# Stage A of a Fourier and MoE kernel by radix 2: folds spread over product groups, burst behind the inverse

## Chip, cores and metric

The kernel runs on one core of a Trainium2 chip. The metric is device time in microseconds (us) of one execution, the median of several runs. An execution has five engines that take their own instructions in order: TensorE (PE in the rows; PEld is its loading of weights), VectorE (DVE), ScalarE (ACT), GpSimd (POOL) and SyncE (SP), which here only issues DMA transfers.

## What is computed

```python
X = np.fft.rfft(x, axis=1)                     # x: 8 batches x 3008 x 256
Yr = Xr @ w_r - Xi @ w_i + b_r
Yi = Xr @ w_i + Xi @ w_r + b_i
Y = softshrink(Yr, 0.01) + 1j * softshrink(Yi, 0.01)
y = np.fft.irfft(Y, n=3008, axis=1)            # 24064 tokens x 256
h = y @ w_in                                   # 256 -> 2048
out = (h * np.cos(h)) @ w_out                  # 2048 -> 256
```

## The kernel before

Every batch of 3008 = 64 x 47 rows goes through a Fourier part and then through the two big products (MoE). The MoE of batch b is 6 tiles of 512 tokens by 16 steps; a step (`moe_step`) makes six matmuls of 512 columns into a PSUM bank `ph` (L937 to L939), passes it through ScalarE and VectorE (`u`, `gh`, `gl`), and three steps later (`SKEW`) `second` makes six more (L919, L920, L923) from `gh` and `gl`. `gl = u - gh` is a subtraction on GpSimd in every second step (`POOL_GL`, L331) and on VectorE in the others (L334).

Between these steps the Fourier part of batch b + 1 is woven in. The generators yield costs in paced units; `pull` takes as many units per step as `share(b)` grants, from sums written out by hand (`COST`, `A_COST`, `LAST`). So the position of each piece is set by the order of the generator `fourier(b)` and by the units of what stands before it. Tile's scheduler then orders each engine's instructions; `floor()` keeps an instruction behind the results of the step before last, and `burst()` keeps the matmuls of one group together and lets the first of them wait for all that the group needs.

One batch's Fourier part runs, for q = 0 to 3, through `combine(q)` (sums and splits into high and low parts), `wmix(q)` (the product with the weights: eight positions, of which six are matmul groups, `pw`, and two are turns, in which VectorE transposes what GpSimd has folded), `forward(q + 1)` (burst `pb`), and `inverse(q - 1)` (burst `pi`, 16 matmuls of 24 rows by 32 columns by 512, each recorded as two passes). At q = 1 to 3 there also stands a group of stage A of the batch after that (`stage_a(b + 1)`, batches 2 to 7, so 18 groups in all): it takes two loads `xt` of 128 x 1024 from DRAM, which GpSimd's queue issues (L448), and does a 64-point transform across partitions.

Stage A before: GpSimd makes for each load a sum `xe` (L460) and, in place, a difference (L461), each 128 x 512. `folds` gives them out after the third position of `wmix`, but without `floor()` for batches over 2, so that the scheduler may run them as early as the load is there. The group (`burst_of`) is a burst `pa` of 8 matmuls of 64 rows by 64 columns by 512 into four PSUM banks; ScalarE copies each bank (`ao`), and SyncE's queue stores them to scratch (L465), from which the next batch's `forward` loads `at` (L565). The four products of one load stand on the four quarters of the 64 x 64 tiles, the two loads one behind the other. The group stands after position 5, the inverse after position 6. Batch 1's stage A runs in another way at the start and is not touched. The constants of stage A are columns 256 to 319 of `ff`.

Of the kernel before, what the change touches and what calls it, by code (L numbers as in the profile page):

```python
# [13 lines left out]
F32 = mybir.dt.float32  # L14
# [73 lines left out]

def _constants():
    n1, s = np.arange(64), np.arange(32)  # L90
# [26 lines left out]
    for sl in range(1, 32):  # L117
        for k2 in range(47):
            sig[sl, k2] = 1 if crt[sl, k2] <= N // 2 else -1
# [61 lines left out]
def tile_body(ctx: ExitStack, tc, x, w_r, w_i, b_r, b_i, w_in, w_out,  # L181
# [26 lines left out]
    def load_constants():  # L208
        with nc.allow_non_contiguous_dma(reason="bias"):
            for r, bsrc in enumerate((b_r, b_i)):  # L210
                nc.gpsimd.dma_start(bb[:, r, :], bsrc.rearrange("(c p) -> p c", p=128))
        ws["sig"] = pool["pro"].tile([96, 32], F32, name="sig", bufs=1)
        nc.gpsimd.dma_start(ws["sig"], c_sig)
        nc.gpsimd.dma_start(fi[0], c_if)
        ws["minus"] = wk.tile([128, 64], F32, tag="xe", name="minus", bufs=2)
        nc.gpsimd.tensor_scalar(out=ws["minus"], in0=ff[:, 256:], scalar1=-1.0, scalar2=None, op0=ALU.mult)
# [223 lines left out]
    def stage_a(b):  # L440
        scr1[b] = dr.tile([2, 24, 32, 2, 256], F32, tag="scr1", name=f"scr1_{b}")
        ld, ev = {}, {}
# [10 lines left out]
        def fold(c):  # L453
            with floor() if b == 2 else ExitStack():
                sums(c)

        def sums(c):
            ev[c] = wk.tile([128, 2, 256], F32, tag="xe", name="xe", bufs=2)
            lo, hi = ld[c][:, :, 0], ld[c][:, :, 1]
            nc.gpsimd.tensor_tensor(out=ev[c], in0=lo, in1=hi, op=ALU.add)  # L460
            nc.gpsimd.tensor_tensor(out=lo, in0=lo, in1=hi, op=ALU.subtract)  # L461

        def store(c, ao, after=None):
            for v in range(2):
                ins = nc.sync.dma_start(  # L465
                    scr1[b][v, 4 * c:4 * c + 4].rearrange("i s r d -> (s r) i d"),
                    ao[64 * v:64 * v + 64].rearrange("p (i d) -> p i d", i=4))
                if after is not None:
                    behind(ins, after.ins, "first tile")
# [7 lines left out]
        def burst_of(cs, banks=None, home=stage_out):  # L477
# [4 lines left out]
            if b == 1:  # L482
                ins = burst(1 if odd else 2, [((p[c, h][64 * v:64 * v + 64], (ws["minus"] if v * g else ff[:, 256:])[64 * h:64 * h + 64],
                            ld[c][64 * h:64 * h + 64, :, g]),
                           dict(start=g == 0, stop=g == 1, skip_group_check=True))
                          for c in cs for g in range(2) for h in range(2) for v in (1, 0)])
                if pro:
                    mark["fill"] = mark["pa"] = ins
            else:
                burst(len(ps2), [((p[c, h][64 * v:64 * v + 64], ff[64 * h:64 * h + 64, 256:320],  # L490
                                   (ld[c][64 * h:64 * h + 64, :, 0] if v else ev[c][64 * h:64 * h + 64])),
                                  dict(start=True, stop=True, skip_group_check=True))
                                 for c in cs for h in range(2) for v in (1, 0)])
            if banks:
                yield 0.0
            for c in cs:
# [11 lines left out]
                if b > 1:  # L508
                    del ld[c], ev[c]
                    load(c + 2)  # L510
            yield BURST

        def folds(j):
            for c in (2 * j, 2 * j + 1):
                fold(c)
                yield 0.5
# [14 lines left out]
        def begin():  # L531
            load(0)
            load(1)

        return SimpleNamespace(begin=begin, folds=folds, alone=alone, release=release, one=lambda *a: burst_of([a[0]], *a[1:]),
                               group=lambda j: burst_of([2 * j, 2 * j + 1]))


    def stage_b(b):
# [15 lines left out]
        def load(q):  # L555
            if b and q < 4:
# [4 lines left out]
                for h in range(4):  # L561
                    own = q == 0 and SLOT0[h] != SLOTS[h]
                    r0 = 64 * (h // 2) + 24 * (h % 2)
                    for (v, r), s0, s1 in ((SLOT0[h], 0, 1), (SLOTS[h], 1, 8)) if own else ((SLOTS[h], 0, 8),):
                        ins = nc.sync.dma_start(t[r0:r0 + 24, 256 * s0:256 * s1].rearrange("j (s d) -> j s d", d=256),  # L565
                                                scr1[b][v, :, 8 * q + s0:8 * q + s1, r])
# [257 lines left out]
    def fourier(b):  # L824
# [14 lines left out]
        if b == 1:  # L839
            yield from quiet()  # L840
            yield from on.forward(1)
        for q in range(4):
            mix = on.wmix(q)
            yield from take(mix, 2)
# [187 lines left out]
    A_COST = 3 * (1.0 + QUIET + 3 * READ + BURST)  # L1032
# [99 lines left out]
```

## Time and profile before

| | us |
|---|---|
| median of 3 runs (2570.58 to 2575.36) | 2571.95 |
| the profiled execution's own time | 2572.61 |
| span of the profiled execution, first to last instruction | 2570.8 |
| TensorE busy | 2548.1 |
| VectorE busy | 1858.0 |
| ScalarE busy | 1676.6 |
| GpSimd busy | 1029.5 |

Busy is the time in which at least one instruction of the engine runs. TensorE's matmuls are pipelined, so two of them overlap in the rows and the distance between starts is what one costs. In rows of busy time by stretch, each engine's us are followed by its count; the granted clock of 1.00 is full speed, and the last two columns are the DMA engines' share and GB/s.

### The profile page before, as it was taken

To read this page: it belongs to the slowest core of one execution; us is meant where nothing else is said; L and a number is where in the kernel's file an instruction comes from. 1 tells how busy PE (TensorE), PEld (TensorE's weight loads), DVE (VectorE), ACT (ScalarE), POOL (GpSimd) and SP (SyncE) were. 2 spreads that over 40 slices of the span, in tenths; PEclk is the share of its full clock that TensorE was granted. 3 is DMA by queue.
4 is the path that set the end of the run, shared out by engine and by line. 5 is a ranking of instruction groups with operands and counts; after the bars stand their busy time and mean duration, and the time that the engine had idled before them with its cause. 6 is when DMAs were issued, how large, how long until landed. Compare 5 with 4: busy or idle time off the path is not lost.

```text
span 2570.8 us, 42992 instructions
## 1 busy us (share of the span) xinstructions
PE 2548.1 (99%) x15961; PEld 2063.0 (80%) x15961; DVE 1858.0 (72%) x2909; ACT 1676.6 (65%) x3119; POOL 1029.5 (40%) x1002
## 2 busy tenths in 40 slices
PE   9999999999999999999999999999999999999999
PEld 7577778877788778887788777887788888888888
DVE  5887776877777777777767777677776777766665
ACT  5766666666666666666666666666676666666666
POOL 2135563555334552345524545244442444322222
PEclk9999999999999999999999999999999999999999
DMA  7545444444335443364423544335433343210000
GB/s 239 185 117 150 133 118 118 128 136 139 91 84 155 133 130 87 90 162 137 120 79 106 146 126 120 98 95 144 140 103 99 90 115 110 65 43 17 17 25 16
DMA packets 172954, 283.12 MB, mean 110 GB/s; under 512 B 15608, under 2 KB 114200, under 8 KB 169160
## 3 DMA queue, kind: packets, MB, share of 16 engines
q1 hardware_dynamic: 161896, 243.78, 33.8%
q0 software_dynamic: 10112, 35.53, 4.4%
q8 instruction: 126, 2.06, 0.3%
q10 hardware_dynamic: 736, 1.05, 0.1%
q14 instruction: 84, 0.69, 0.1%
HBM read 149.76 MB, written 130.55 MB: 109 GB/s over the span
## 4 chain that ended last, share of the span: by engine, by line
PE 84%; DVE 5%; DMA 3%; ACT 3%; issue 3%; POOL 2%; SPq 0%; ACTq 0%; DVEq 0%; POOLq 0%
PE ph L937 12%; PE po L919 12%; PE po L923 12%; PE po L920 12%; PE ph L938 12%; PE ph L939 12%; PE pw L676 2%; PE pw L678 2%; PE pw L677 2%; PE pc L383 1%; PE pb L383 1%; DVE u L951 1%; DMA xt<-in_dram 1%; PE pw L672 1%; DVE u L948 1%
## 5 line engine op out<-in xcount | busy, mean ns | idle before, releaser
L331 POOL TENSOR_TENSOR gl<-u,gh 128x512 fp32r<-128x512 f32 (+1 forms) x384 | 493.0, 1284 | 1088.6 <-ACT gh L952 931.7
L950 ACT ACTIVATE u<-u 128x512 f32<-128x512 f32 (+1 forms) x768 | 478.6, 623 | 351.2 <-DVE u L948 350.3
L948 DVE SCALAR_TENSOR_TENSOR u<-ph,u 128x512 f32<-128x512 f32 (+1 forms) x768 | 515.4, 673 | 263.8 <-ACT u L947 261.7
L951 DVE TENSOR_TENSOR u<-ph,u 128x512 f32<-128x512 f32 (+1 forms) x768 | 518.5, 675 | 246.6 <-ACT u L950 234.7
L952 ACT CAST gh<-u 128x512 fp32r<-128x512 f32 (+1 forms) x768 | 467.8, 609 | 214.7 <-DVE u L951 211.0
L947 ACT ACTIVATE u<-ph 128x512 int32<-128x512 f32 (+1 forms) x768 | 448.4, 586 | 244.1 <-PE ph L939 234.3
L937 PE MATMUL ph<-xTh,win 128*128 128x512 f32 (+1 forms) x1536 | 600.9, 391 | 0.0
L919 PE MATMUL po<-gh,wout 128*128 128x512 f32 (+1 forms) x1536 | 599.1, 390 | 1.5 <-ACT gh L952 1.2
L938 PE MATMUL ph<-xTl,win 128*128 128x512 f32 (+1 forms) x1536 | 594.0, 387 | 0.0
L939 PE MATMUL ph<-xTh,win 128*128 128x512 f32 (+1 forms) x1536 | 593.5, 386 | 0.0
L920 PE MATMUL po<-gh,wout 128*128 128x512 f32 (+1 forms) x1536 | 593.0, 386 | 0.0
L923 PE MATMUL po<-gl,wout 128*128 128x512 f32 (+1 forms) x1536 | 476.6, 388 | 7.8 <-POOL gl L331 7.4
L334 DVE TENSOR_TENSOR gl<-u,gh 128x512 fp32r<-128x512 f32 (+1 forms) x384 | 308.4, 803 | 74.3 <-ACT gh L952 66.5
L937 PEld LDWEIGHTS ph<-xTh,win 128*128 128x128 f32 x1536 | 288.2, 188 | 87.4 <-issue 22.4
L923 PEld LDWEIGHTS po<-gl,wout 128*128 128x128 f32 x1536 | 287.1, 188 | 70.8 <-POOL gl L331 10.8
L919 PEld LDWEIGHTS po<-gh,wout 128*128 128x128 f32 x1536 | 288.2, 188 | 67.3 <-ACT ao L499 8.1
L939 PEld LDWEIGHTS ph<-xTh,win 128*128 128x128 f32 x1536 | 288.4, 188 | 56.2
L938 PEld LDWEIGHTS ph<-xTl,win 128*128 128x128 f32 x1536 | 288.4, 188 | 50.7
L920 PEld LDWEIGHTS po<-gh,wout 128*128 128x128 f32 x1536 | 288.5, 188 | 50.4
L676 PE MATMUL pw<-Xh,wf 128*128 128x384 f32 x336 | 114.4, 340 | 2.5 <-ACT Xh L613 2.3
L716 POOL TENSOR_TENSOR odd<-st 128x184 f32<-128x184 f32 (+1 forms) x112 | 68.1, 609 | 119.8 <-DVE st L693 104.3
L678 PE MATMUL pw<-Xl,wf 128*128 128x384 f32 x336 | 113.3, 340 | 0.2 <-POOL Xl L331 0.2
(119 smaller groups left out, 2453.0 us busy)
## 6 DMA issues: line engine op xcount, KB each, us to landing
scrF<-at SPq DMA_DIRECT2D x28, 1024.0 KB
z<-scrF SPq DMA_DIRECT2D x112, 256.0 KB
scrT<-tr SPq DMA_DIRECT2D x56, 512.0 KB
y<-scrT SPq DMA_DIRECT2D x112, 256.0 KB
bt<-scr SPq DMA_DIRECT2D x94, 256.0 KB
scr<-bo SPq DMA_DIRECT2D x224, 96.0 KB
scr<-ao SPq DMA_DIRECT2D x80, 256.0 KB
out_dram<-ob SPq DMA_DIRECT2D x80, 256.0 KB
```

What stands on the lines that cost most here:

```text
L331: return nc.gpsimd.tensor_tensor(out=lo, in0=x, in1=hi.bitcast(F32), op=ALU.subtract)
L919: mm(po[e][:, :n], wo[0][:, 0, f, es], gh[:, :n], start=f == 0, stop=False)
L920: mm(po[e][:, :n], wo[0][:, 1, f, es], gh[:, :n], start=False, stop=False)
L923: mm(po[e][:, :n], wo[0][:, 0, f, es], gl[:, :n], start=False, stop=f == NFC - 1)
L937: mm(h, win[:, 0, c, fs], th[:, c, :n], start=c == 0, stop=False)
L938: mm(h, win[:, 0, c, fs], tl[:, c, :n], start=False, stop=False)
L939: ins = mm(h, win[:, 1, c, fs], th[:, c, :n], start=False, stop=c == 1)
L947: nc.scalar.activation(k[:, :n], h, AF.Identity, bias=0.25, scale=1.0 / TWO_PI)
L948: nc.vector.scalar_tensor_tensor(out=u[:, :n], in0=h, scalar=1.0 / TWO_PI, in1=k[:, :n], op0=ALU.mult, op1=ALU.subtract)
L950: nc.scalar.activation(u[:, :n], u[:, :n], AF.Sin, bias=HALF_PI, scale=TWO_PI)
L951: product = nc.vector.tensor_tensor(out=u[:, :n], in0=h, in1=u[:, :n], op=ALU.mult)
L952: step = [nc.scalar.copy(gh[:, :n], u[:, :n])]
```

## The change

The 64-point transform is split once more. Per load GpSimd now makes four operations of 128 x 512 instead of two: sum and difference of the two halves into a new tile `t` (one buffer of twice the size in place of two buffers `xe`), then sum and difference of these back into the load's tile. The host orders the input's rows so that the pairs meet, and orders the constants by even and odd outputs (`_order`). The burst (`octet`) has 16 matmuls of 32 rows by 32 columns by 512 instead of 8 of 64 by 64; both loads stand side by side in the columns. The banks are copied as before and stored with as many transfers of the same size, in another layout of the scratch.

The folds are given out one by one behind the positions of `wmix` by the table `FOLDS` (one load's four at q = 0, one at q = 1, two loads' eight at q = 2 and at q = 3, all before the inverse), each with `floor()` and a cost of 0.5 units. The first matmul of the burst waits for the last fold of both loads. The group is placed one position later, after position 6, and the inverse one earlier, after position 5. `A_COST` and `LAST` rise accordingly.

```diff
-QUIET, READ, BURST, LAST = 3.0, 1.1, 2.5, 21.0
+QUIET, READ, BURST, LAST = 3.0, 1.1, 2.5, 24.0
+FOLDS = (1, 1, 0, 0, 1, 1, 0, 0), (1, 1, 1, 1, 0, 0, 0, 0), (2, 2, 2, 1, 1, 0, 0, 0), (2, 2, 2, 1, 1, 0, 0, 0)
+FOLD = 0.5
...
-        def sums(c):
-            ev[c] = wk.tile([128, 2, 256], F32, tag="xe", name="xe", bufs=2)
-            lo, hi = ld[c][:, :, 0], ld[c][:, :, 1]
-            nc.gpsimd.tensor_tensor(out=ev[c], in0=lo, in1=hi, op=ALU.add)
-            nc.gpsimd.tensor_tensor(out=lo, in0=lo, in1=hi, op=ALU.subtract)
+        def folds():
+            for c in range(6):
+                one, two = ld[c][:, :, 0], ld[c][:, :, 1]
+                t = wk.tile([128, 2, 2, 256], F32, tag="xe", name="xe", bufs=1)
+                for j, (out, in0, in1) in enumerate(((t[:, 0], one, two), (t[:, 1], one, two),
+                                                     (ld[c][:, 0], t[:, :, 0], t[:, :, 1]),
+                                                     (ld[c][:, 1], t[:, :, 0], t[:, :, 1]))):
+                    with floor():
+                        done[c] = nc.gpsimd.tensor_tensor(out=out, in0=in0, in1=in1, op=ALU.subtract if j % 2 else ALU.add)
+                    yield FOLD
...
-                burst(len(ps2), [((p[c, h][64 * v:64 * v + 64], ff[64 * h:64 * h + 64, 256:320],
-                                   (ld[c][64 * h:64 * h + 64, :, 0] if v else ev[c][64 * h:64 * h + 64])),
-                                  dict(start=True, stop=True, skip_group_check=True))
-                                 for c in cs for h in range(2) for v in (1, 0)])
...
+        def octet(j):
+            cs = (2 * j, 2 * j + 1)
+            p = some("pa", 4)
+            burst(4, [((p[k][64 * c + 32 * w:64 * c + 32 * w + 32],
+                        ff[32 * k:32 * k + 32, 256 + 32 * w:288 + 32 * w],
+                        ld[cs[c]][32 * k:32 * k + 32, :, w]),
+                       dict(start=True, stop=True, skip_group_check=True))
+                      for c in range(2) for w in range(2) for k in range(4)], [done[c] for c in cs])
...
+        def woven(q):
+            for i, c in enumerate(on.wmix(q)):
+                yield c
+                if more:
+                    yield from take(a.folds, FOLDS[q][i])
+                yield None
...
         for q in range(4):
-            mix = on.wmix(q)
-            yield from take(mix, 2)
+            mix = woven(q)
+            yield from run(mix, 2)
             if q < 3 and (q or b > 1):
                 yield from quiet()
                 yield from on.forward(q + 1)
-            yield from take(mix, 1)
-            if q and more:
-                yield from a.folds(q - 1)
-            yield from take(mix, 2)
+            yield from run(mix, 3)
+            if q:
+                yield from quiet()
+                yield from on.inverse(q - 1)
+            yield from run(mix, 1)
             if q and more:
                 yield from quiet()
                 yield from a.group(q - 1)
-            yield from take(mix, 1)
-            if q:
-                yield from quiet()
-                yield from on.inverse(q - 1)
-            yield from mix
+            yield from run(mix, 9)
...
-    A_COST = 3 * (1.0 + QUIET + 3 * READ + BURST)
+    A_COST = 3 * (8 * FOLD + QUIET + 3 * READ + BURST)
```

## Rows read from the trace of the kernel before

**Rows 1.** The page's first part: busy time, share of the span, instructions by engine.

```profile
PE 2548.1 (99%) x15961; PEld 2063.0 (80%) x15961; DVE 1858.0 (72%) x2909; ACT 1676.6 (65%) x3119; POOL 1029.5 (40%) x1002
```

**Rows 2.** TensorE's timeline around one burst pa: start, duration, instruction, count.

```profile
632.99 0.39 PE L923 MATMUL po<-gl,wout 128*128 128x512 f32 x1
633.30 0.64 PE L373 MATMUL pa<-xt,ff 64*64 64x512 f32 x1
...
634.66 0.59 PE L383 MATMUL pa<-xe,ff 64*64 64x512 f32 x1
...
635.52 0.40 PE L919 MATMUL po<-gh,wout 128*128 128x512 f32 x1
```

**Rows 3.** The same view: around the next burst pi; first and last of five waits.

```profile
374.42 0.73 PE L923 MATMUL po<-gl,wout 128*128 128x512 f32 x2 [0.67 <-POOL gl L331]
...
643.67 0.39 PE L920 MATMUL po<-gh,wout 128*128 128x512 f32 x1
...
644.35 0.61 PE L923 MATMUL po<-gl,wout 128*128 128x512 f32 x2
...
644.90 0.70 PE L383 MATMUL pi<-y,iw 24*32 24x512 f32 x15
...
645.36 0.68 PE L383 MATMUL pi<-y,iw 24*32 24x512 f32 x15
...
646.30 0.40 PE L938 MATMUL ph<-xTl,win 128*128 128x512 f32 x1
...
648.14 0.39 PE L920 MATMUL po<-gh,wout 128*128 128x512 f32 x1
649.55 0.73 PE L923 MATMUL po<-gl,wout 128*128 128x512 f32 x2 [1.02 <-POOL gl L331]
...
1594.38 0.73 PE L923 MATMUL po<-gl,wout 128*128 128x512 f32 x2 [2.07 <-POOL gl L331]
```

**Rows 4.** Waits of TensorE over the span: total us, times, longest.

```profile
PE po L923 <- POOL gl L331: 7.4, 6, 2.1
```

**Rows 5.** GpSimd's timeline at the same place as rows 3.

```profile
636.87 1.13 POOL L448 DMA_DIRECT2D xt<-in_dram  x2
641.46 1.29 POOL L460 TENSOR_TENSOR xe<-xt 128x512 f32<-128x512 f32 x1 [3.47 <-DMA xt<-in_dram]
...
646.91 1.36 POOL L706 TENSOR_TENSOR st<-st,sgn 128x384 f32<-128x384 f32 x1
648.23 1.27 POOL L331 TENSOR_TENSOR gl<-u,gh 128x512 fp32r<-128x512 f32 x1
```

**Rows 6.** Groups by shape, GpSimd: count, busy us, mean ns, idle before.

```profile
L461 POOL TENSOR_TENSOR xt<-xt 128x512 f32<-128x512 f32 x36 | 49.9, 1390 | 2.4
L460 POOL TENSOR_TENSOR xe<-xt 128x512 f32<-128x512 f32 x36 | 49.3, 1372 | 47.6 <-DMA xt<-in_dram 46.1 <-PE ph L939 1.4
```

**Rows 7.** Windows in q = 2 and 3: busy PE, PEld, DVE, ACT, POOL; clock; DMA.

```profile
873.70:892.60 18.90, 18.90 (x111) 15.40 (x110) 15.54 (x26) 11.10 (x21) 7.80 (x9) 1.00 0.20 72
933.10:948.60 15.50, 15.50 (x73) 13.09 (x72) 11.16 (x20) 9.46 (x18) 9.35 (x9) 1.00 0.31 69
```

**Rows 8.** GpSimd's timeline in that q = 3: one subtraction gl.

```profile
945.32 1.29 POOL L331 TENSOR_TENSOR gl<-u,gh 128x512 fp32r<-128x512 f32 x1
```

**Rows 9.** TensorE's timeline: the matmul that uses it.

```profile
948.34 0.39 PE L923 MATMUL po<-gl,wout 128*128 128x512 f32 x1
```

**Rows 10.** One line's instructions, VectorE: count, ns minimum/median/maximum, first and last start.

```profile
L334 DVE TENSOR_TENSOR gl<-u,gh x384: 615/692/1796, 121.4 to 2564.9; 128x512 fp32r<-128x512 f32 x160, 128x448 fp32r<-128x448 f32 x32
```

**Rows 11.** SyncE's queue in that q = 3: start, duration, DMA issues.

```profile
933.54 1.81 SPq L731 DMA_DIRECT2D y<-scrT  x4
...
954.32 4.08 SPq L465 DMA_DIRECT2D scr<-ao  x4
961.21 3.64 SPq L565 DMA_DIRECT2D at<-scr  x6
```

**Rows 12.** Busy time as in rows 7, ahead of that inverse.

```profile
942.00:946.00 4.00, 4.00 (x20) 3.47 (x19) 2.71 (x6) 2.03 (x4) 1.79 (x3) 1.00 0.00 0
```

More of the change, by code (lines that the diff above doesn't have):

```diff
@@ L440, in stage_a @@
     def stage_a(b):
-        scr1[b] = dr.tile([2, 24, 32, 2, 256], F32, tag="scr1", name=f"scr1_{b}")
-        ld, ev = {}, {}
+        scr1[b] = dr.tile([24, 2, 32, 2, 256], F32, tag="scr1", name=f"scr1_{b}")
+        ld, done = {}, {}
         def load(c):
@@ L481, in burst_of @@
             p = {(c, h): ps2[2 * (c - cs[0]) + h] for c in cs for h in range(2)}
[L482 to L489, printed above, removed]
[L490 to L493 removed]
+            ins = burst(1 if odd else 2, [((p[c, h][64 * v:64 * v + 64], (ws["minus"] if v * g else ff[:, 256:])[64 * h:64 * h + 64],
+                        ld[c][64 * h:64 * h + 64, :, g]),
+                       dict(start=g == 0, stop=g == 1, skip_group_check=True))
+                      for c in cs for g in range(2) for h in range(2) for v in (1, 0)])
+            if pro:
+                mark["fill"] = mark["pa"] = ins
             if banks:
@@ L507, in burst_of @@
                     store(c, ao)
-                if b > 1:
-                    del ld[c], ev[c]
-                    load(c + 2)
             yield BURST
[L513 to L516, printed above, removed]
+        def octet(j):
[6 more added lines that the diff above has]
+                      for c in range(2) for w in range(2) for k in range(4)], [done[c] for c in cs])
+            for h in range(2):
+                ao = stage_out("ao")
+                for i in range(2):
+                    drained(p[2 * h + i], nc.scalar.copy(ao[:, 512 * i:512 * i + 512], p[2 * h + i]))
+                    if h == 0 or i == 0:
+                        yield Hold(READ)
+                for c in range(2):
+                    n = 4 * cs[c] + 2 * h
+                    nc.sync.dma_start(
+                        scr1[b][n:n + 2].rearrange("j v s r d -> (s r) (j v) d"),
+                        ao[64 * c:64 * c + 64].rearrange("p (x d) -> p x d", x=4))
+                del ld[cs[h]]
+                load(cs[h] + 2)
+            yield BURST
         def alone():
@@ L533, in begin @@
             load(1)
-        return SimpleNamespace(begin=begin, folds=folds, alone=alone, release=release, one=lambda *a: burst_of([a[0]], *a[1:]),
-                               group=lambda j: burst_of([2 * j, 2 * j + 1]))
+        return SimpleNamespace(begin=begin, folds=folds(), alone=alone, release=release, one=lambda *a: burst_of([a[0]], *a[1:]),
+                               group=octet)
     def stage_b(b):
@@ L841, in fourier, with run @@
             yield from on.forward(1)
+        def woven(q):
[4 more added lines that the diff above has]
+                yield None
+        def run(gen, n):
+            while n:
+                c = next(gen, 0)
+                if c == 0:
+                    break
+                if c is None:
+                    n -= 1
+                else:
+                    yield c
         for q in range(4):
-            mix = on.wmix(q)
-            yield from take(mix, 2)
+            mix = woven(q)
+            yield from run(mix, 2)
             if q < 3 and (q or b > 1):
@@ L1113 @@
     xp = np.ascontiguousarray(xp).reshape(NB, 128, 24 * D)
+    pairs = xp[2:].reshape(NB - 2, 2, 64, 6, 2, 2, D)
+    rows = (np.arange(32)[:, None] + 32 * np.arange(2)) % 64
+    parted = [pairs[:, :, :, :, i][:, :, (rows + 32 * i) % 64].transpose(0, 1, 2, 4, 5, 3, 6) for i in range(2)]
+    xp[2:] = np.stack(parted, 2).reshape(NB - 2, 128, 24 * D)
     consts = _constants()
```

15 lines of the change are left out of this document (7 added, 8 removed).

## Prediction

> **What bounds the kernel now.** I read the page's first part first: TensorE is busy for 2548.1 of 2570.8 us, GpSimd for 1029.5, VectorE for 1858.0 [rows 1]. Nothing but TensorE's own stream can bound this kernel over most of its length, and the two things that can shorten it are matmul time taken out and waits of TensorE taken out. For the first I read TensorE's timeline by starts, since ends overlap. An ordinary 512-column matmul of the MoE costs about 0.227 us: from 643.67 to 644.35 three are started [rows 3]. For the second I read the waits of TensorE: its matmuls waited 7.4 us in 6 waits for a `gl` that GpSimd makes, the longest 2.1 us [rows 4]. Everything else of GpSimd, VectorE and the queues is covered by TensorE, as long as it is in time.
>
> **The burst: removed work on the path.** Around a burst `pa` the MoE matmul before it starts at 632.99 and the second one behind it at 635.52 [rows 2]. Of these 2.53 us two ordinary pitches are 0.45, so the burst costs 2.08 us. Inside it four waves are to be seen, two passes for each load, and they start between 633.30 and 634.66 [rows 2]: four products run side by side, and the second load waits for the first. The new burst's shape, 16 products of 32 by 32 tiles and 512 columns in four banks, is not in the trace of before for stage A, but the inverse's burst `pi` has 16 products on the same 16 places with 24 rows in place of 32. It shows 15 and 15 instructions in two waves, at 644.90 and 645.36. From the first of the two L923 at 644.35 to L938 at 646.30 are 1.95 us, less three pitches (0.68), so it costs 1.27 us [rows 3]. Rows of the moving operand lie across partitions, so 32 should cost what 24 do. I take 1.27. The bounds are 1.27 and 2.08 (nothing runs more side by side than now). The saving is 0.81 us a group, and 6 batches x 3 groups make 18: **14.6 us**. The number of bank copies, of their turns in the list and of switches between tile shapes stays, so nothing is added there.
>
> **The folds: removed waits.** GpSimd runs its queue in order. In q = 3 its row shows the loads for the next batch issued at 636.87, a wait of 3.47 us for their landing, four folds in one run from 641.46 on, the inverse's first operation at 646.91, and only then a `gl` at 648.23 to 649.50 [rows 5]. TensorE had started L920 at 648.14 and could start L923, which reads that `gl`, only at 649.55, having waited 1.02 us [rows 3]. The folds of the next batch stood there because without `floor()` they were ordered as early as their load allowed. Five of the six waits of [rows 4] stand right behind such a run, one in each q = 3 that has a next batch's loads behind it, from 0.67 us at 374.42 to 2.07 at 1594.38 [rows 3]. With `floor()` on every fold the run goes away, and so does the wait for the landing. Each wait also costs 0.16 us more than its idle time shows (648.14 to 649.55 is 1.41, less 0.227 and 1.02). Five such tails are 0.8 us, and the sixth wait is smaller than the average, so I take the row's whole 7.4 as what goes: **7.4 us**. What is late next in these places is nothing of GpSimd, since its queue there is then empty but for the two load issues of 1.13 us [rows 5].
>
> **The folds: added work.** 6 batches x 6 loads x 2 more operations are 72 more on GpSimd, at the mean of today's 1372 and 1390 ns [rows 6]: 1.38 us each, 99 us in all. Its sum of 1029.5 then is 1129 of about 2556. Over the span that is covered. By stage it is not everywhere. The folds of two loads, 8 x 1.38 = 11.0 us, stand behind positions 1 to 5 at q = 2 and q = 3. In the stretch of q = 2 GpSimd is busy for 7.80 of 18.90 us today, with no fold in it, and in that of q = 3 for 9.35 of 15.50 [rows 7]. Either stretch runs from the start of the second position to the end of the fifth and the pause after it. At q = 3 these are three positions of 3.5 units, a turn of 1.2, the old folds' 1.0 and the pause of 3.0, 15.7 units in 15.5 us: a unit is about 1 us here. The eight folds add 4 units and the old folds' 1.0 go, so 3 us come to each stretch. At q = 2 that is 18.8 us of work in 21.9, which has room. At q = 3 it is 20.4 in 18.5: GpSimd is full for this stretch, and the operations queue. Who suffers is `gl`, of which GpSimd makes three in such a stretch. One of them ends at 946.61 [rows 8] and is used at 948.34 [rows 9]: 1.73 us of margin. Two folds ahead of it (2.76 us) would make TensorE wait 1.03 us. Lower bound: nothing, since `floor()` puts a pair of folds right behind a `gl` and the next on GpSimd is two steps away. Upper bound: all three are late, 3.1 us for each of six q = 3, 18.6 us. I take one late `gl` per q = 3, nearer to the lower end because the queue overflows by 1.9 us alone: **6.2 us**.
>
> VectorE's `gl` of the other steps reads two SBUF operands, and takes 615 to 1796 ns with a median of 692 [rows 10]. Long ones fall where GpSimd is busy. VectorE has 713 us of idle time [rows 1], so I cost this at nothing; its bound is inside the 18.6. The Trainium skill (GPSIMD Engine Reference, Specifications and Engine selection) speaks against the change here: GpSimd shares its SBUF interfaces with VectorE, and elementwise work of two inputs belongs on VectorE. The spread of that row agrees. By the rule each of the 72 added folds could stretch one such operation by up to 1.1 us, 79 us of VectorE, which fits into its idle time; the sum would be the same.
>
> **The burst's new wait.** The burst's first matmul waits for the last fold of both loads, and behind it in TensorE's order stands all the MoE. The last fold is given out after position 5; the inverse (8.8 units with its pause) and a position of 3.5 lie between, some 12 us at 1 us a unit, against an overflow of 1.9 us. I cost it at 0; the cover is these 12 us, and without them it costs the overflow, 1.9 us at each of six q = 3.
>
> **What is moved.** The inverse moves one position up and no longer stands behind the group, some 11 us in all. Its loads `y` are issued at 933.54 [rows 11], and the DMA engines are idle between 942 and 946 [rows 12], so they have landed by then, while the earlier place is near 948.5. That leaves over 6 us at q = 3, the tightest. SyncE's queue now takes the inverse's stores first and then the four of the group, which stand at 954.32 today, and the loads `at` at 961.21 that read them [rows 11] come as much later; their burst opens only the batch after. On GpSimd's queue the loads `xt` move with the group. They land within some 4.6 us of issue (636.87 to 641.46) [rows 5], and between the group and the first fold of the next q lie a whole `combine`, 11 units, and two positions. Nothing is charged for these. `LAST` and `A_COST` make the list some 4% longer and its units run that much faster, which moves pieces by a step and costs nothing by itself.
>
> **Sum.** Against the profiled execution's own 2572.6 us: 2572.6 - 14.6 - 7.4 + 6.2 = 2556.8. The median of before is 0.7 lower, so 2556 us, 0.6% faster.
>
> **Rivals.**
> - *No new wait.* TensorE's order hides the late `gl`, and small waits elsewhere go too: 2572 - 14.6 - 7.4 = 2550, less up to 3 is 2547. For it: the queue overflows by 1.9 us only. Against it: margins of 1.7 us where folds of 1.4 come in pairs.
> - *GpSimd is full.* At q = 3 every `gl` is late, with VectorE's slowed ones besides: +18.6 instead of +6.2, 2568 to 2569. For it: 20.4 us of work in 18.5. Against it: folds queue only when given out, and most of that queue is over before the group.
> - *The burst waits for the folds: slower.* TensorE stands still in order at each of the 18 bursts until the last fold is done. It decides from 22.0 / 18 = 1.2 us a burst. If the last two folds (2.76 us) are ordered right ahead of each burst, that is 49.7 less 22.0, near 2600. Against it: the 12 us between.
> - *The 16 products don't run side by side.* The burst stays at 2.08 us: 2572 - 7.4 + 6.2 = 2571, no change. Against it: the two waves of [rows 3].
>
> **How the numbers follow.** A measurement of this kernel tells about 0.2% (5 us) from no change, so faster is below 2566.8. Forecast, 2550 to 2563: 0.52. No new wait, 2546 to 2550: 0.17. GpSimd full, 2563 to 2571: 0.18, a third of it still faster. Slower: 0.08. Not side by side: 0.05. Faster is 0.52 + 0.17 + 0.06 = 0.75, same 0.12 + 0.04 = 0.16, slower 0.09. The range from 2546 to 2571 takes in all but the slower case and some of the edges.
>
> **What would show it.** In the profile after: the burst `pa` as 16 and 16 instructions in two waves, with the same 1.27 us between its neighbours; no run of four folds behind the inverse, and no wait of L923 there; GpSimd near 1129 us busy, near full in q = 3, with waits of L923 for `gl` of about 1 us there. I am wrong if TensorE shows a wait of `pa` for folds, a wait of `pi` for its loads, or waits of L923 that sum to more than some 13 us.

## The result

The changed kernel takes 2587.17 us (median; 2586.26 to 2587.32) beside 2571.26 us of the kernel before, a ratio of 1.0058 (95% interval 1.0043 to 1.0073): by that ratio **slower by 15 us**, where 2556 was forecast, 15 us faster. The first part of the page after answers [rows 1]:

```profile
PE 2540.3 (98%) x16249; PEld 2060.5 (80%) x16249; DVE 1866.1 (72%) x2909; ACT 1672.4 (65%) x3119; POOL 1130.4 (44%) x1074
```

GpSimd's 1130.4 us are the 1129 that were forecast, and TensorE is busy 7.8 us less. But the span is 14.4 us longer (2585.2), so TensorE's idle time has doubled, from 22.7 to 44.9 us. The waits of TensorE over the span (total us, times, longest) answer [rows 4]:

```profile
PE ph L969 <- DVE u L983: 22.0, 22, 2.3
PE pi L380 <- DMA y<-scrT: 5.3, 1, 5.3
...
PE po L955 <- POOL gl L338: 0.4, 2, 0.2
```

The waits for GpSimd's `gl` are gone (7.4 to 0.4 us), as forecast. In their place stands a wait that has no row in the kernel before: `ph` waits 22 times for VectorE's product `u` (L983), the last reader of the PSUM bank that `ph` wants. Twelve of these waits (13.4 us) follow a group's burst `pa` within 4 us, and ten (8.6 us) follow an inverse's burst `pi`, which the change didn't shorten. And one inverse waits 5.3 us for its loads `y`. TensorE's timeline around one burst `pa` (start, duration, instruction, count, idle before and releaser) answers [rows 2]:

```profile
1287.70 0.61 PE L955 MATMUL po<-gl,wout 128*128 128x512 f32 x2
1288.25 0.61 PE L380 MATMUL pa<-xt,ff 32*32 32x512 f32 x1
1288.26 0.70 PE L390 MATMUL pa<-xt,ff 32*32 32x512 f32 x15
1288.70 0.59 PE L380 MATMUL pa<-xt,ff 32*32 32x512 f32 x1
1288.71 0.68 PE L390 MATMUL pa<-xt,ff 32*32 32x512 f32 x15
1290.71 0.50 PE L969 MATMUL ph<-xTh,win 128*128 128x512 f32 x1 [1.32 <-DVE u L983]
```

The burst is the two waves that were forecast. Where no wait follows, it costs 1.27 us, worked out as from [rows 2] (the median of the 18 is 1.58, waits with it). Here 1.32 us of waiting stand right behind it, more than the 0.81 that it saves.

The other engines in the same stretch show where the product was so late. VectorE's timeline:

```profile
1273.08 0.99 DVE L741 STREAM_TRANSPOSE tr<-odd 128x256 f32<-128x256 f32 x2 [0.32 <-POOL odd L733]
1274.00 0.65 DVE L983 TENSOR_TENSOR u<-ph,u 128x512 f32<-128x512 f32 x1
1275.34 1.30 DVE L341 TENSOR_TENSOR gl<-u,gh 128x512 fp32r<-128x512 f32 x1 [0.69 <-ACT gh L984]
...
1282.93 1.28 DVE L763 TENSOR_TENSOR bo<-pi,bo 128x512 f32<-128x512 f32 x2
1284.13 1.27 DVE L764 TENSOR_TENSOR bo<-pi,bo 128x512 f32<-128x512 f32 x2
1285.33 0.68 DVE L980 SCALAR_TENSOR_TENSOR u<-ph,u 128x512 f32<-128x512 f32 x1
...
1286.70 0.69 DVE L983 TENSOR_TENSOR u<-ph,u 128x512 f32<-128x512 f32 x1 [0.17 <-ACT u L982]
...
1288.58 0.69 DVE L980 SCALAR_TENSOR_TENSOR u<-ph,u 128x512 f32<-128x512 f32 x1 [0.72 <-ACT u L979]
1289.97 0.69 DVE L983 TENSOR_TENSOR u<-ph,u 128x512 f32<-128x512 f32 x1 [0.70 <-ACT u L982]
```

ScalarE's:

```profile
1287.43 0.62 ACT L984 CAST gh<-u 128x512 fp32r<-128x512 f32 x1 [0.34 <-DVE u L983]
1287.96 0.59 ACT L979 ACTIVATE u<-ph 128x512 int32<-128x512 f32 x1
```

GpSimd's:

```profile
1269.64 2.87 POOL L468 TENSOR_TENSOR xt<-xe 128x512 f32<-128x512 f32 x2
1272.47 1.12 POOL L733 TENSOR_TENSOR odd<-st 128x184 f32<-128x184 f32 x2
...
1274.80 2.98 POOL L468 TENSOR_TENSOR xe<-xt 128x512 f32<-128x512 f32 x2
```

Read it as a chain. A bank of `ph` comes free through four instructions by turns: ScalarE's `u` (L979), VectorE's (L980), ScalarE's (L982), VectorE's product (L983). From 1287.96 to 1290.66 that is 2.70 us, in which neither engine is full; each waits for the other. Over the span these waits of VectorE are (total us, times, longest):

```profile
DVE u L983 <- ACT u L982: 248.8, 417, 1.0
DVE u L980 <- ACT u L979: 244.4, 316, 5.8
DVE gl L341 <- ACT gh L984: 78.2, 138, 0.9
```

The group holds four of the six banks (`BANKS`), so two are left for `ph`, and TensorE runs at the speed of this chain. The chain began late. The inverse's sums `bo` held VectorE from 1282.93 on, so that `u` (L980) began at 1285.33; its product came at 1286.70, the cast `gh` behind it at 1287.43, and only then, in ScalarE's order, the next step's `u` at 1287.96.

Some 14 us earlier the folds had made VectorE's work late: `odd` began behind two on GpSimd's queue, the transpose `tr` waited for `odd` and stood ahead of the product (1274.00) in VectorE's order, and `gl` beside the next folds took 1.30 us in place of 0.69. What this costs at the bursts is left to the experiments.

### The profile page after: what moved, and what is told of

Read it like the earlier page. It is cut to its first block, busy times and chain, and to the rows that moved or that the text cites. A ratio compares the mean times of both kernels' runs of the same rounds, so it can differ in the third digit from the quotient of the medians.

```text
span 2585.2 us, 43668 instructions
## 1 busy us (share of the span) xinstructions
PE 2540.3 (98%) x16249; PEld 2060.5 (80%) x16249; DVE 1866.1 (72%) x2909; ACT 1672.4 (65%) x3119; POOL 1130.4 (44%) x1074
## 4 chain that ended last, share of the span: by engine, by line
PE 51%; DVE 6%; ACT 4%; POOL 3%; issue 2%; DMA 0%; SPq 0%; ACTq 0%; DVEq 0%; POOLq 0%
PE ph L969 8%; PE po L951 8%; PE ph L970 7%; PE ph L971 7%; PE po L952 7%; PE po L955 7%; DVE u L983 2%; ACT u L982 1%; ACT gh L984 1%; DVE u L980 1%; PE pw L693 1%; PE pw L695 1%; PE pw L694 1%; PE pc L390 1%; POOL xe L468 1%
## 5 line engine op out<-in xcount | busy, mean ns | idle before, releaser
L982 ACT ACTIVATE u<-u 128x512 f32<-128x512 f32 (+1 forms) x768 | 478.5, 623 | 397.5 <-DVE u L980 396.8
L983 DVE TENSOR_TENSOR u<-ph,u 128x512 f32<-128x512 f32 (+1 forms) x768 | 518.5, 676 | 259.3 <-ACT u L982 248.8
L980 DVE SCALAR_TENSOR_TENSOR u<-ph,u 128x512 f32<-128x512 f32 (+1 forms) x768 | 514.0, 672 | 248.0 <-ACT u L979 244.4
L979 ACT ACTIVATE u<-ph 128x512 int32<-128x512 f32 (+1 forms) x768 | 448.4, 586 | 207.2 <-PE ph L971 200.7
L341 DVE TENSOR_TENSOR gl<-u,gh 128x512 fp32r<-128x512 f32 (+1 forms) x384 | 320.5, 835 | 83.9 <-ACT gh L984 78.2
L955 PEld LDWEIGHTS po<-gl,wout 128*128 128x128 f32 x1536 | 287.1, 188 | 70.9 <-issue 14.6
L693 PE MATMUL pw<-Xh,wf 128*128 128x384 f32 x336 | 115.0, 342 | 1.4 <-DVE u L983 1.3
L694 PE MATMUL pw<-Xh,wf 128*128 128x384 f32 x336 | 113.3, 337 | 0.0
```

What stands on the lines that cost most here:

```text
L955: mm(po[e][:, :n], wo[0][:, 0, f, es], gl[:, :n], start=False, stop=f == NFC - 1)
L979: nc.scalar.activation(k[:, :n], h, AF.Identity, bias=0.25, scale=1.0 / TWO_PI)
L980: nc.vector.scalar_tensor_tensor(out=u[:, :n], in0=h, scalar=1.0 / TWO_PI, in1=k[:, :n], op0=ALU.mult, op1=ALU.subtract)
L982: nc.scalar.activation(u[:, :n], u[:, :n], AF.Sin, bias=HALF_PI, scale=TWO_PI)
L983: product = nc.vector.tensor_tensor(out=u[:, :n], in0=h, in1=u[:, :n], op=ALU.mult)
```

## The experiments

Each ratio is against the kernel before on the same chip. Beside the ratio I use the length of each MoE batch in the profiled run: the time from the first matmul that reads `gl` in one batch to the same in the next, worked out from TensorE's timeline. Batches 0 to 5 hold the 18 groups, batch 0 with the start. Behind them nothing differs: batch 6 is 302.9 us in every run.

| kernel | median, us | ratio (95%) | batch 0, us | batches 1 to 5, us |
|---|---|---|---|---|
| before | 2571.26 | | 320.0 | 1570.6 |
| after | 2587.17 | 1.0058 (1.0043 to 1.0073) | 331.3 | 1573.0 |
| e1 half the folds | 2566.84 | 0.9984 (0.9975 to 0.9993) | 327.7 | 1555.4 |
| e6 spread, place, pace | 2562.94 | 0.9965 (0.9952 to 0.9978) | 324.6 | 1555.9 |
| e11 = e6, `at` behind `y` | 2559.68 | 0.9958 (0.9941 to 0.9974) | 321.8 | 1556.1 |
| e16 = e11, short burst | 2560.51 | 0.9958 (0.9943 to 0.9973) | 321.8 | 1557.3 |
| e18 = e11, half sums | 2559.78 | 0.9955 (0.9940 to 0.9970) | 321.8 | 1555.5 |
| e17 = e11, both | 2546.75 | 0.9902 (0.9887 to 0.9916) | 319.7 | 1545.3 |

**Taking the change apart.** e1 leaves out the second pair of GpSimd's operations per load:

```diff
-                    with floor():
-                        done[c] = nc.gpsimd.tensor_tensor(out=out, in0=in0, in1=in1, ...)
+                    if j % 2:
+                        with floor():
+                            done[c] = nc.gpsimd.tensor_tensor(out=t[:, int(j == 1)], in0=one, ...)
```

> The changed kernel with two of the four GpSimd operations of every load left out (the second pair in effect; the burst reads what is there, so stage A of batches 2 to 7 is not the transform). Burst, waits, places and paced units stay. Theory 1 (the 72 added operations fill GpSimd and hold VectorE up, whose late products keep the PSUM banks that the next ph needs): GpSimd falls from 1130 to some 1030 us, the 22.0 us of waits of ph for u go to under 8, the time falls by 12 to 18 us to 2569 to 2575. Theory 2 (the inverse's sums on VectorE right ahead of the group's burst): the waits right behind the group's burst stay, and the time falls by less than 6 us.

It came to 2566.84 us, a little below the range of theory 1, and TensorE's main wait falls from 22.0 to:

```profile
PE ph L970 <- DVE u L984: 5.1, 11, 1.3
```

So the second pair costs 0.74% or 19 us. e6 goes the other way: the kernel before with its two folds and its long burst, but with the spread, the new place and the new pace.

```diff
+FOLDS = (1, 0, 0, 0, 1, 0, 0, 0), (1, 0, 1, 0, 0, 0, 0, 0), (1, 1, 1, 1, 0, 0, 0, 0), (1, 1, 1, 1, 0, 0, 0, 0)
+FOLD = 1.0
...
-    A_COST = 3 * (1.0 + QUIET + 3 * READ + BURST)
+    A_COST = 3 * (4 * FOLD + QUIET + 3 * READ + BURST)
```

> The kernel before with its own two folds per load and its own burst of 8 products, but with the folds spread over the positions, each held behind the results of the step before last, and with the order and the pace of the changed kernel; no radix 2. If the spread does what the prediction said (the waits of po for GpSimd's gl go, 7.4 us) and the order and the pace cost nothing: 2562 to 2566 us. If the new order and pace bring the drift of the first two batches by themselves (some 4 at the start, some 8 at batch 1's last inverse), as the half-fold run's wait of 4.5 us for the inverse's loads suggests: 2572 to 2577 us, with a wait of pi for y of about 5 us.

2562.94 us, as its first theory has it. From here the change falls into three steps, by the ratios: spread, place and pace together -9.0 us (before to e6), the shorter burst, with the folds in other slots, +4.9 (e6 to e1), the added folds +19.0 (e1 to after). Each ratio is known to 0.001 or 0.0015, so each step to some 4 us. Of the 4.9, batch 0 has 3.1, where the wait for `y` is longer too. The burst, which carried the forecast, brings nothing. e7 tries it in the kernel before, alone:

```diff
-                burst(len(ps2), [((p[c, h][64 * v:64 * v + 64], ff[64 * h:64 * h + 64, 256:320], ...
+                burst(len(ps2), [((ps2[k][64 * i + 32 * v:64 * i + 32 * v + 32], ff[32 * k:32 * k + 32, 256 + 32 * v:288 + 32 * v], ...
```

> The kernel before with nothing changed but the matmuls of the group: 16 products of 32 by 32 in place of 8 of 64 by 64, on the data of the two old folds (the second butterflies are left out, so stage A of batches 2 to 7 is not the transform). If the burst's saving of 0.81 us x 18 reaches the end: 2556 to 2559 us. If a burst that is over sooner only brings the next wait forward (TensorE then waits for gl, u or the banks): 2563 to 2571 us, with the waits of TensorE up by what is missing.

2576.46 us, a ratio of 1.0021 (1.0012 to 1.0031), above both ranges. The bursts `pa` cost 1.27 us, and the waits have grown, from 7.4 us for `gl` and no row of `ph`:

```profile
PE po L923 <- POOL gl L331: 12.0, 13, 3.0
PE ph L937 <- DVE u L951: 6.2, 9, 1.4
```

**Why the burst brings nothing.** e16 is e7's edit on e11, the fastest kernel, which has no such waits; e17 also leaves out the second of the inverse's two sums on VectorE; e18 leaves it out with the long burst.

```diff
-                nc.vector.tensor_tensor(out=near, in0=even, in1=far, op=ALU.add)
-                drained(p[2 * r], nc.vector.tensor_tensor(out=far, in0=even, in1=far, op=ALU.subtract))
+                drained(p[2 * r], nc.vector.tensor_tensor(out=near, in0=even, in1=far, op=ALU.add))
```

> The fastest kernel so far (spread alone, at behind y, 2559.7 us) with the burst of 16 products of 32 by 32 on the two old folds (the second butterflies are left out, so stage A is not the transform). The prediction's term: -14.6, 2545 us. Theory G: most of it comes back as waits of ph for VectorE behind the bursts; 2554 to 2560 us, with these waits at 5 us or more where there are none now.

> The same, with the second of the inverse's two sums left out on VectorE as well. Theory G: with VectorE's stream shortened ahead of the group the burst's saving reaches the end, 2544 to 2549 us. Rival, that the saving is lost to something that VectorE's stream doesn't set: within 2 us of the run with the short burst alone.

> The fastest kernel so far (2559.7 us, long burst, spread alone) with the second of the inverse's two sums left out on VectorE, so half of the outputs are not written. Theory G says that with the burst of 2.08 us VectorE's chain is in time already: 2557 to 2560 us, and the 13 us between the runs with the short burst are the burst's saving set free. Rival, that leaving out the sums gains by itself, whatever the burst: 2545 to 2550 us.

The burst alone: 2560.51 us, no change (the ratio of e11 and of e16 is 0.9958). The sums alone: 2559.78, no change. Both: 2546.75, that is 13 us less, near the whole forecast of 14.6; batches 2 to 4 go from 311.0 us each to 308.6, which is the 3 x 0.81 us of their bursts. The wait of TensorE for VectorE in e16:

```profile
PE ph L960 <- DVE u L974: 8.4, 14, 1.6
```

and in e17:

```profile
PE ph L959 <- DVE u L973: 0.9, 3, 0.3
```

So TensorE and VectorE's chain are both limits there, within less than 0.81 us of each other. Leaving out the second sum also frees the inverse's bank one sum earlier, but no wait of TensorE in e16 is for `bo`, so it is the product that comes in time. The 8.4 us in e16 are some 60% of what didn't come; a wait also costs around itself (from the `ph` below at 1267.21 to the next matmul at 1267.55 are 0.34 us, not 0.227), and I took the rest no further apart. In e16 VectorE shows it (the product that the next `ph` waits for ends at 1267.15, and the idle times are those of the chain):

```profile
1259.42 1.28 DVE L753 TENSOR_TENSOR bo<-pi,bo 128x512 f32<-128x512 f32 x2
1260.62 1.28 DVE L754 TENSOR_TENSOR bo<-pi,bo 128x512 f32<-128x512 f32 x2
...
1266.46 0.69 DVE L974 TENSOR_TENSOR u<-ph,u 128x512 f32<-128x512 f32 x1 [0.70 <-ACT u L973]
```

TensorE in e16, behind the burst of 1265.68:

```profile
1267.21 0.50 PE L960 MATMUL ph<-xTh,win 128*128 128x512 f32 x1 [0.39 <-DVE u L974]
```

e13 leaves the same sums out of the changed kernel:

> The changed kernel, with the second of the two sums (the subtraction of 0.68 us) that VectorE makes of each bank pair of the inverse left out, so half of the outputs are not written: 2.5 us of VectorE become 1.3 us between the inverse and the group, 56 x 0.68 = 38 us in all. Theory G, that the chain of u over VectorE is what TensorE waits for around the bursts: the waits of ph for VectorE fall from 22.0 to 10 us or less and the time is 2570 to 2577 us. Rival, that VectorE has 28% of idle time and these sums are off the path: 2583 to 2588 us.

2568.04 us, a ratio of 0.9986 (0.9976 to 0.9995), so 0.72% or 19 us less for 27 us of busy time (1866.1 to 1839.4) of an engine that is idle 28% of the span. Theory G was near: the time is just below its range, the wait just above. The wait of `ph` for VectorE (22.0 before the edit):

```profile
PE ph L968 <- DVE u L982: 11.5, 12, 1.6
```

**How the added folds cost.** e12 puts writes of zeros of about the same time in place of the second pair. Writes read nothing, so they stand in GpSimd's queue without reading beside VectorE.

```diff
-                        done[c] = nc.gpsimd.tensor_tensor(out=out, in0=in0, in1=in1, ...)
+                        if j < 2:
+                            done[c] = nc.gpsimd.tensor_tensor(out=out, in0=in0, in1=in1, ...)
+                        else:
+                            nc.gpsimd.memset(t[:, j - 2], 0.0)
+                            nc.gpsimd.memset(out[:, 0], 0.0)
+                            done[c] = nc.gpsimd.memset(out, 0.0)
```

> The changed kernel, but the second pair of folds of each load is replaced by writes of zeros of about the same time on GpSimd (three short ones for each, 1.0 to 1.5 us together), so stage A is not the transform; order, dependencies and places stay. They read nothing. Theory E, that the second pair costs by stretching VectorE's gl while both read (gl of 0.69 us takes 1.3 to 1.8): gl on VectorE falls back near 825 ns on average and the time is 2567 to 2574 us. Theory F, that it costs by its place in GpSimd's queue (odd and st late, and so the turn and the product behind it on VectorE): the waits of ph for VectorE stay near 20 us and the time is 2582 to 2588 us.

2580.04 us, a ratio of 1.0042 (1.0028 to 1.0055): between the two theories. By the groups of VectorE's `gl` by shape (count, busy us, mean ns, idle before), the added stretching is gone in e12 (e1, without a second pair, has a mean of 825 ns):

```profile
L341 DVE TENSOR_TENSOR gl<-u,gh 128x512 fp32r<-128x512 f32 x320 | 262.1, 819 | 78.4 <-ACT gh L989 71.0 <-PE po L960 0.7 <-PE ph L976 0.7
```

where the changed kernel has

```profile
L341 DVE TENSOR_TENSOR gl<-u,gh 128x512 fp32r<-128x512 f32 x320 | 279.9, 875 | 77.7 <-ACT gh L984 72.3
```

The Trainium skill (SBUF — State Buffer, Who interferes with whom) says that a VectorE instruction with two SBUF inputs contends with a GpSimd instruction that reads SBUF and not with one that only writes it; these two rows agree. By the ratios e12 is 4 us faster than the changed kernel (the intervals overlap), by the profiled batches 7. That is not the stretching's share. The writes are some 6 us shorter in sum (97.5 against 103.2 us), and TensorE's clock was lower in e12: its mean granted clock is 0.997 in the profiled execution, against 0.999 in the changed kernel. One minus this mean, times the span, is an estimate of what the lower clock took at most, so e12 lost some 5 us more by it. Against e1, which has nothing in place of the second pair, e12 is 15 us slower (1.0042 against 0.9984), some 5 of them by the clock. So work in GpSimd's queue costs even where it reads nothing; how the 19 us divide between the queue and the stretching stays open.

e9 gives the eight folds out four at a time, ahead of the inverse:

```diff
-FOLDS = ..., (2, 2, 2, 1, 1, 0, 0, 0), (2, 2, 2, 1, 1, 0, 0, 0)
+FOLDS = ..., (4, 4, 0, 0, 0, 0, 0, 0), (4, 4, 0, 0, 0, 0, 0, 0)
```

> The changed kernel, but at q = 2 and q = 3 the eight folds are given out four at a time behind the first two positions, away from the inverse and the group. Theory D, that the added folds cost where a burst holds four of six banks and the chain of u is what TensorE waits for: the waits of ph for VectorE fall from 22.0 to 12 us or less and the time is 2570 to 2577 us. Rival, that they cost wherever they stand, by their sum on GpSimd: the waits only move (to gl, as in the kernel before, or to u at an earlier place) and the time is 2582 to 2590 us.

2597.03 us, a ratio of 1.0107 (1.0092 to 1.0123), above both ranges. Theory D fails: the waits of `ph` for the product are 20.9 us, and 7.9 us of waits of `ph` for VectorE's transposes `at` (L603) are new. The folds stand in runs of four here, so the price of nearness by itself is not shown, and most of the 10 us more than in the changed kernel are, by the same estimate, the clock's (0.996). GpSimd in e9:

```profile
1276.78 2.97 POOL L468 TENSOR_TENSOR xe<-xt 128x512 f32<-128x512 f32 x2
1279.71 0.57 POOL L733 TENSOR_TENSOR odd<-st 128x184 f32<-128x184 f32 x1
```

and VectorE:

```profile
1280.32 0.45 DVE L741 STREAM_TRANSPOSE tr<-odd 128x256 f32<-128x256 f32 x1 [1.10 <-POOL odd L733]
1280.69 0.65 DVE L983 TENSOR_TENSOR u<-ph,u 128x512 f32<-128x512 f32 x1
```

`odd` waits for two folds, VectorE stands 1.10 us in order for `odd`, and the product that frees a bank is behind it.

e5 moves the second pair to VectorE (`nc.vector if j > 1 else nc.gpsimd`):

> The changed kernel, but of the four folds of a load the second pair runs on VectorE, so GpSimd has as much to do as before the change (near 1030 us busy) and VectorE 72 operations of about 0.7 us more (near 1900 to 1920 us). Theory A, that the added folds cost by running on GpSimd beside VectorE's two-operand work and stretching it: TensorE's waits of ph for VectorE fall from 22.0 to near 5 us, and the time is 2566 to 2573 us, close to the run with half the folds. Theory B, that any added work ahead of u on the way to the bank ph costs, whichever engine does it: the waits of ph for VectorE stay at 15 us or more and the time is 2580 to 2590 us.

2606.41 us, a ratio of 1.0134 (1.0119 to 1.0149), above both ranges. The waits of `ph` for VectorE are 25.4 us, so theory A fails, and what theory B says of the waits holds: work ahead of the product costs on whichever engine. That it costs most on VectorE is not shown. VectorE is busy 61 us more than in e1 (1908.8 against 1848.0) and the time is 1.5% or 39 us longer, but the mean granted clock is 0.991 here and 0.999 in e1. By the same estimate that is some 20 us: half of the 39, and about all that e5 takes more than the changed kernel (19 us, at 0.999 too).

**Place and pace.** The prediction cost both at nothing. e2 restores the order (group behind position 5, inverse behind 6), e3 the two numbers of pace, e10 and e14 are e6 with both restored and with the pace alone restored, e15 is the kernel before with the new pace alone.

```diff
-QUIET, READ, BURST, LAST = 3.0, 1.1, 2.5, 24.0
+QUIET, READ, BURST, LAST = 3.0, 1.1, 2.5, 21.0
-    A_COST = 3 * (8 * FOLD + QUIET + 3 * READ + BURST)
+    A_COST = 3 * (1.0 + QUIET + 3 * READ + BURST)
```

> The changed kernel with the group put back after position 5 and the inverse after position 6; four folds, table and wait of the burst for them stay. Theory 2 (the new order costs): the waits of ph right behind the group's burst, 1 to 2.5 us each, go, and so does the 5.3 us wait of the inverse for y in batch 1; the time falls by 12 to 18 us. Theory 1 (the folds cost, whatever the order): the ph waits stay at some 20 us, and the burst itself begins to wait for folds; only the y wait of some 8 us with its slow clock goes, time 2576 to 2582.

> The changed kernel with the sums that set the pace as before (LAST 21.0, 1.0 for the folds in A_COST); nothing else. Theory 4 (the higher share alone costs the 3 to 4 us by which the first tile of batch 0 is later, and squeezes the inverse of batch 1): the drift against the kernel before at the end of the first tile falls from 3.7 us to under 1, time 2580 to 2584. If pace is nothing: within 3 us of 2587.

> The kernel before with only the folds spread and held behind the results of the step before last; its burst, its order (group ahead of the inverse) and its pace are kept. If the 9 us that the spread alone with the new place gained come from the spread: 2560 to 2565 us, with no wait of po for GpSimd's gl above 2 us. If the new place has a part in it: 2566 to 2571 us.

> The spread-alone kernel (2562.9 us) with the pace of the kernel before, the new place kept. With old place and old pace the spread came to 2576.9. If the pace makes the difference, as it did in the changed kernel (12 us): 2574 to 2580 us. If the place does: 2561 to 2566 us.

> The kernel before with nothing changed but its two numbers of pace (LAST 24 in place of 21, and 3 units more for each group in A_COST). If the pace costs nothing by itself, as the prediction put it: 2569 to 2575 us. If it sets where bursts fall against the MoE step, which is worth 12 us and 24 us in two other kernels: outside of that, and the direction is not foretold; by the other two runs it would gain, 2555 to 2566 us.

| kernel | place | pace | ratio (95%) |
|---|---|---|---|
| before | old | new (e15) | 1.0039 (1.0027 to 1.0052) |
| before and spread | old | old (e10) | 1.0024 (1.0015 to 1.0033) |
| before and spread | new | old (e14) | 1.0059 (1.0042 to 1.0075) |
| before and spread | new | new (e6) | 0.9965 (0.9952 to 0.9978) |
| after | old | new (e2) | 1.0062 (1.0047 to 1.0077) |
| after | new | old (e3) | 1.0117 (1.0100 to 1.0134) |
| after | new | new | 1.0058 (1.0043 to 1.0073) |

Four of the five runs fell outside every range set for them, and e15 lost time where the runs before it had spoken for a gain. e2 shows how: the waits of `ph` for the product went from 22.0 to 1.6 us, as its theory 2 had it, but `po` then waited 14.7 us for ScalarE's `gh` and `pa` 5.3 us for the folds.

No column has a price of its own. The new pace costs 10 us in the kernel before, whose runs of folds then stand worse, and brings 24 us in the spread one. What moves are waits, and with them TensorE's clock (0.996 on average in e14's profiled execution, 0.999 in e6's, some 8 us of the 24 by the estimate). e15:

```profile
PE po L923 <- POOL gl L331: 13.1, 7, 3.1
```

e10, where `gl` is no longer waited for but the inverse is:

```profile
PE pi L375 <- DVE u L972: 7.9, 5, 1.6
```

e14:

```profile
PE pa L375 <- DVE u L972: 10.3, 7, 1.9
```

**The one late inverse.** In the changed kernel batch 1's last inverse waits 5.3 us for `y`, until 405.67. SyncE's queue there (start, duration, issues):

```profile
390.01 2.41 SPq L582 DMA_DIRECT2D at<-scr  x6
392.46 0.38 SPq L742 DMA_DIRECT2D scrT<-tr  x1
398.32 1.78 SPq L748 DMA_DIRECT2D y<-scrT  x4
```

Six loads `at` of the next batch stand ahead of the store of `tr` and the loads `y` that read it. e4 moved the loads `at` in the generator's order; e8 and e11 hold them behind the loads `y`:

```diff
+            mark["y"] = Y[q][1][-1]
...
-            stages[b + 1].load(0)
+            with tc.issue_after(mark["y"].ins) if b == 1 else ExitStack():
+                stages[b + 1].load(0)
```

> The changed kernel with the loads at for batch 2 issued behind the last inverse of batch 1 instead of ahead of its pauses, for batch 1 only. Theory 3 (SyncE's queue: the loads at wait there for the group's stores, and the stores tr and loads y of the inverse stand behind them): the 5.3 us wait of pi for y and the half clock behind it go, time falls by 8 us to 2579. Rival: y is late because the whole list of batch 1 ends later and the transfers themselves take that long; then the wait stays above 3 us.

> The changed kernel, but in batch 1 the loads at of the next batch are issued on SyncE's queue behind the loads y of the last inverse, where before the scheduler had put them ahead. Theory C, that the at loads hold up the inverse's store and loads on that queue: the wait of pi for y (5.3 us) and the half clock behind it go, and the time is 2577 to 2581 us. Rival: what is late is the turn on VectorE ahead of the store; then y still waits for 3 us or more and the time stays at 2584 to 2588 us.

> The spread-alone kernel (old folds, old burst, new place and pace), and in batch 1 the loads at behind the loads y, as in the run that took 5 us off the changed kernel. Its wait of pi for y (2.5 us) goes: 2558 to 2561 us. If that wait is covered by something else that is late: 2562 to 2564 us.

e4 is inconclusive: the scheduler issued the loads in the old place, the wait (5.1) stayed, and so did the time (2586.0). e8 moved them: 2582.09 us, a ratio of 1.0040 (1.0025 to 1.0055), just above theory C's range, and the wait is

```profile
PE pi L380 <- DMA y<-scrT: 0.3, 1, 0.3
```

With it, batch 0 of the changed kernel goes from 331.3 to 323.8 us; batches 1 to 5 took 3.5 us back (1573.0 to 1576.5), for which the clock is shown at the end. e11, the same edit on e6, came to 2559.68 us (0.9958): it beats both kernels, and it has neither radix 2 nor the short burst.

## Why the prediction was wrong

- **The burst, -14.6.** The cost (1.27 us) was right; the step that failed is "Nothing but TensorE's own stream can bound this kernel over most of its length". At the bursts the chain of `u` is next, by less than 0.81 us. I took TensorE's few waits [rows 4] to mean that the rest is in time, without asking by how much. On the spread kernel the term measured nothing (e11 to e16: +0.8 us by the medians, 0.0 by the ratios), and -13.0 by the medians once VectorE was in time (e18 to e17).
- **The waits for `gl`, -7.4.** They went. But the term isn't the spread's own: with old place and pace the waits for `gl` are gone (0.5 us) and the time is 6 us longer (e10). Spread, place and pace together gave 9.0.
- **The added folds, +6.2.** GpSimd's sum was right, and so was that it is full in q = 3 (busy 15.76 of the 15.80 us from 1266.70 in the rows above). The price was sought in the wrong place: in GpSimd's own `gl`, which TensorE waited for less than ever. It came through VectorE, by `odd` and by the stretched `gl`, at 19 us, near the 18.6 of the bound. The step that failed is "VectorE has 713 us of idle time [rows 1], so I cost this at nothing": that idle time is mostly ScalarE's turn in the chain, not room. Of VectorE's 719 idle us in the changed kernel 571 are the three waits for ScalarE shown above. The prediction had named the Trainium skill (GPSIMD Engine Reference, Specifications and Engine selection) against the change, and set this idle time against it. The shared interfaces show in VectorE's `gl` (819 ns in e12, 875 in the changed kernel). One operation was shorter on VectorE (987 ns in e5 against 1451 on GpSimd), as the Trainium skill has it, and the kernel was no faster for it.
- **The burst's new wait, 0.** Right: `pa` waits for no fold. In e2, where the group stands one position earlier, it does, for 5.3 us in 9 waits.
- **The moves, 0.** The margin of `y` was taken from a q = 3 in the middle (over 6 us); batch 1's last inverse, behind other loads on SyncE's queue, had none, and e8 gave 5 us back (2587.17 to 2582.09). "Costs nothing by itself" of the pace was wrong by 10 us (e15), and by 24 us the other way in the spread kernel (e14 to e6).
- **The rivals.** The 19 us are nearest to "GpSimd is full" in size, but not in its mechanism. "A wait of `pi` for its loads" was on the list of signs; the wait of `ph` for VectorE, the largest, was not.

The forecast's sum was -15.8 and +14.9 was measured (by the ratio): the burst is 19.5 of the 30.7 us between them, the folds are 12.8, and the waits for `gl` with place and pace -1.6.

What stays open is how the 19 us of the folds divide between GpSimd's queue and the stretched `gl`, and how the place and the pace set each single wait: the runs show that these trade against each other, not a rule for where a burst should stand.

## What to carry to other kernels

Before matmul time is taken out of a stretch, measure there how long ahead of the matmul that follows its bank or operand was ready: a saving is worth no more than that margin, and in a chain that goes back and forth between two engines neither is busy and both are late. Work added to an engine off the path costs what it delays in the in-order queues that it feeds, so follow each neighbour in its queue to the next product that frees a buffer. In a schedule woven by hand, order and pace are part of the change and have no price of their own; try them together with it. Before the time of a run is put down to work or waits, look at its granted clock.

## What the hardware showed

TensorE's clock falls to its lower level (1.2 GHz) behind some waits of a few us. Windows of the changed kernel behind the wait of 5.3 us (columns as in [rows 7]):

```profile
408.20:411.50 3.30, 3.30 (x10) 2.93 (x9) 2.48 (x5) 1.24 (x3) 0.00 (x0) 0.50 0.11 25
```

and of e5, behind a wait of 3.18 us at 1288.39:

```profile
1289.00:1293.60 4.60, 4.60 (x12) 3.62 (x11) 3.22 (x7) 2.72 (x5) 1.27 (x1) 0.50 0.28 114
```

The granted clock is 0.50 in both, and in both TensorE had stood in the wait named just before; in the first, the matmuls of 448 columns start 0.37 us apart, more than the 0.227 of 512 columns in [rows 3]. So a wait can be paid twice: this one took 7.5 us of batch 0 (331.3 against e8's 323.8), not 5.3.

The length of a wait alone doesn't tell whether the clock falls behind it. In the changed kernel a wait of 2.28 us ends at 662.61, and the clock stays:

```profile
659.00:666.00 7.00, 4.72 (x48) 3.01 (x17) 4.51 (x6) 4.47 (x9) 3.37 (x4) 1.00 0.14 41
```

In e8 the same wait of 2.28 us ends at 654.04, and the clock falls behind it, as behind one of 2.07 us in batch 2 (0.50 too; 1.00 in the changed kernel):

```profile
655.30:658.50 3.20, 3.20 (x9) 2.47 (x8) 0.68 (x2) 2.49 (x6) 1.79 (x2) 0.50 0.00 0
```

Batches 1 and 2 of e8 are 1.8 and 1.6 us longer than in the changed kernel, which is what batches 1 to 5 took back there.
